# Strided attention in blocks of 18 tokens, V cast straight to its place, x turned on chip

## The chip, the cores and the metric

The kernel runs on one core of one Trainium2 chip. The core has five engines that run at the same time, each through its own instruction stream in order: PE (TensorE, matrix products into PSUM), DVE (VectorE), ACT (ScalarE), POOL (GpSimd) and SP (SyncE). They meet only through semaphores. SP and POOL compute nothing here: they issue DMAs. The metric is the device time in microseconds of one launch, as the median of several runs.

## The reference

An attention with two kinds of sparse masks, and after it a two-layer MLP with a rational function between the layers. There are 8 sequences (batches) of 576 tokens, 8 heads of 64 columns.

```python
stride = 32
scores = scale * np.matmul(q, k.transpose(0, 1, 3, 2))      # 8 x 8 x 576 x 576
rel = pos[:, None] - pos[None, :]
mask_local = (rel >= 0) & (rel < stride)                    # heads 0 to 3
mask_strided = (rel >= 0) & (pos[None, :] % stride == pos[:, None] % stride)   # heads 4 to 7
attn = softmax(np.where(mask, scores, -1e9))
x = (attn @ v) with heads side by side                      # 4608 x 512
h = x @ w_in                                                # 4608 x 2048
P = a[0] + a[1] * h + a[2] * h**2 + a[3] * h**3
Q = 1.0 + np.abs(b[0]) * np.abs(h) + np.abs(b[1]) * h**2
out = (P / (Q + 1e-06)) @ w_out                             # 4608 x 512
```

In a strided head, token t sees only tokens t, t - 32, t - 64 and so on: for each remainder of t by 32 there is a small attention of its own over 18 tokens.

## The kernel before

The program is written as a list of operations, each with an engine, a guessed duration, a key (its due time) and the tiles that it reads and writes. `schedule()` (line 124) places them in order of key on a model of the five engines, the PSUM banks and one DMA pipe, and so fixes each engine's stream; `emit()` (line 211) turns the dependences into semaphore waits. A DMA on SP or POOL that must wait holds all that stands behind it in that engine's stream.

For each batch b there are these stages.

- `casts(b)` (line 423, seven POOL DMAs): q, k and v are read as f32 and written as bf16 into DRAM. Local heads go in pairs to `lq16` and `lk16` (L428, 1,152 pieces of 128 B each), strided heads to `sq16` and `sk16` and all of v to `v16` (L436, long rows). The casts of b + 2 are released (`after`) by the first transpose of b + 1.
- `loads(b)` (line 464, on SP): four DMA transposes bring q and k into SBUF with the head dimension on partitions (`lqT`, `lkT` L469, `sqT`, `skT` L475). Then six loads put V for local heads into `vL` (L481, L486) and eight put V for strided heads into `vS` (L495), each of 36 partitions x 16 pieces of 128 B. `vL` and `vS` have a column of ones, so that AV also gives the row sum.
- `attention(b)`, local: a mask matmul (L509), 72 small score matmuls (L522), row maxima on DVE (L546), their subtraction by matmul (L553), exp on ACT to `pL` (L559, L563), a DMA transpose to `ptL` on SP (L566), 72 AV matmuls (L635).
- `attention(b)`, strided, two heads at a time (`j2`): blocks of 36 tokens, that is, remainders by 16, half of whose entries are masked. Mask (L578), 32 score matmuls of 64 x 36 (L591), maxima (L601), subtraction (L608), exp to `pS` (L614), transpose to `ptS` (L619); then 64 AV matmuls with P stationary (L687).
- `norm` (L655, L658) divides by the sums from PSUM into `xl` (local) and `xS` (strided). Stores from SP write these to `xs16` in DRAM (L665, L669, L696), and `gather` (L711) transposes them back into `xt`, a ring of two tiles of 512 tokens.

The MLP runs over nine chunks of 512 tokens (`mlp`, line 719). Each has 64 matmuls of 128 x 512 with W_in (L731), evacuated by ACT (L735) into two groups `h`; on each group |h| on ACT (L746) or DVE (L750), six bf16 passes on DVE (L753, L755, L768 to L776), Ln and Exp for the quotient on ACT (L759, L764); then 64 matmuls with W_out (L789), evacuated by ACT (L795) and stored by SP (L801).

The order at the start is casts(0), both halves of W_in, casts(1), both halves of W_out, all on POOL's queue without a wait between them. Attention of batch b has key 33 b - 20 and the MLP of chunk c key 33 c + 10, so attention(b + 1) is spread into mlp(b). After batch 7 two chunks, 7 and 8, are left with no attention beside them.

Of the kernel before, what the change touches and what calls it, by code (L numbers as in the profile page):

```python
# [305 lines left out]
def bass_strided_sparse_attn__then__act_rational_pade_kernel(nc, q, k, v, moe_w_in, moe_w_out, moe_a, moe_b, out):  # L306
# [59 lines left out]
    R_ptS = ring("ptS", 2, [128, 8, 112])  # L366
    R_xl = ring("xl", 1, [128, NLS])
    R_xS = ring("xS", 1, [128, 2048])
    R_ng = ring("ng", 4, [128, 18])
    R_rc = ring("rc", 4, [128, 18], f32)  # L370
    R_xt = ring("xt", 2, [128, NK1, CH])
# [51 lines left out]
    def casts(b, key, after=()):  # L423
        for t in (T_lq[b], T_lk[b], T_sq[b], T_sk[b], T_v[b]):
            t.new()

        def local(pair, s_t, d_t, t):
            P.op("pool", lambda e: e.dma_start(  # L428
                d_t[b, pair, :, :].rearrange("s (hh d) -> s hh d", hh=2),
                s_t[b, 2 * pair:2 * pair + 2, :, :].rearrange("hh s d -> s hh d")),  # L430
                2.8, key, w=[t], dma=(1.2, 3.0), after=after)

        def bulk(s_t, d_t, h0, nh, hd, t):
# [12 lines left out]
        bulk(v, vs, 0, H, H, T_v[b])  # L446

    def weights_in(i, key):
# [5 lines left out]
            2.8, key, w=[T_win[i]], dma=(5.5, 3.0))  # L454

    def weights_out(i, key, after=()):
# [4 lines left out]
            3.1, key, w=[T_wout[i]], dma=(5.5, 3.0), after=after)  # L461


    def loads(b, key):
        st = {}
        for nm, R, d_t, T in (("lq", R_lq, lq, T_lq), ("lk", R_lk, lk, T_lk)):
# [4 lines left out]
                1.25, key, r=[T[b]], w=[t], dma=(1.2, 2.2))  # L471
        for nm, R, d_t, T in (("sq", R_sq, sq, T_sq), ("sk", R_sk, sk, T_sk)):
# [4 lines left out]
                1.25, key + 0.1, r=[T[b]], w=[t], dma=(1.2, 2.2))  # L477
        vl = R_vL.next()
        st["vl"] = vl
        for hh in range(2):  # L480
            P.op("sp", lambda e, hh=hh: e.dma_start(  # L481
                vl.t[64 * hh + 32:64 * hh + 64, :, 0, 0:64],
                bass.AP(tensor=vs, offset=(b * H + hh) * S * D, ap=[[D, 32], [2 * S * D, 2], [1, D]])),
                0.5, key + 0.2, r=[T_v[b]], w=[vl], dma=(0.05, 2.0))
            for pair in range(2):
                P.op("sp", lambda e, hh=hh, pair=pair: e.dma_start(  # L486
                    vl.t[64 * hh:64 * hh + 64, pair, 1:NB, 0:64],
                    bass.AP(tensor=vs, offset=(b * H + 2 * pair + hh) * S * D,
                            ap=[[D, 64], [LB * D, NB - 1], [1, D]])),
                    0.5, key + 0.2, r=[T_v[b]], w=[vl], dma=(0.6, 2.0))  # L490
        vS = R_vS.next()
        st["vS"] = vS
        for r in range(2):
            for h in range(HL):
                P.op("sp", lambda e, r=r, h=h: e.dma_start(  # L495
                    vS.t[64 * r:64 * r + CS, h, :, 0:64],
                    bass.AP(tensor=vs, offset=(b * H + HL + h) * S * D, ap=[[16 * D, CS], [D, 16], [1, D]])),
                    0.7, key + 0.3, r=[T_v[b]], w=[vS], dma=(0.35, 2.0))
        return st


    def attention(b, st, key):
# [63 lines left out]
        P.op("sp", lambda e: e.dma_start_transpose(ptL.t[:, :, :], ppL.t[:, 0:NLS]), 1.25, key, r=[ppL], w=[ptL],  # L566
             dma=(1.1, 2.0))


        ptS = []  # L570
        for j2 in range(2):
            ky = key + 4 + 4 * j2
            SS = Banks(2)

            def smask(e, SS=SS):
                r = None
                for j in range(2):
                    r = e.matmul(bank(SS, 512 * j, 8 * CS), IDN[:, :],  # L578
                                 MS[:, :].unsqueeze(1).broadcast_to([128, 8, CS]),
                                 start=True, stop=False, skip_group_check=True)  # L580
                return r
            P.op("pe", smask, 0.25, ky, r=[T_c], w=[SS])

            def sscore(e, SS=SS, j2=j2):
                r = None
                for j in range(2):
                    h = 2 * j2 + j
                    for r2 in range(8):
                        for par in range(2):
                            p = 64 * par  # L590
                            r = e.matmul(bank(SS, 512 * j + CS * r2, CS, p, p + CS),  # L591
                                         sqt.t[p:p + 64, h, r2:S // 2:8], skt.t[p:p + 64, h, r2:S // 2:8],
                                         start=False, stop=True, skip_group_check=True)
# [276 lines left out]
```

## Time and profile before

| | us |
|---|---|
| Median of 3 runs | 594.68 |
| Lowest, highest | 588.09, 608.74 |
| The profiled execution | 588.41 |
| Its span in the trace | 586.60 |
| PE busy in the span | 349.3 |
| DVE busy | 314.7 |
| ACT busy | 306.6 |
| Moved by DMA | 62.71 MB in 213,187 packets |

The span runs from the first to the last instruction of the trace; 1.8 us of the measured time lie outside it. In the page's line of slices each digit is the busy share of a fortieth of the span in tenths. A row of a group gives line, engine, operation, output and inputs, shapes and count; then busy time, mean ns of one, and the idle time before it with what ended it. Matmuls overlap, so a group's busy time divided by its count says what one costs in a row. "SPq" is time in which SP's queue is issuing. The DMA share of a window can be over 1, since packets of two queues on one DMA engine overlap.

### The profile page before, as it was taken

The page shows a single profiled execution, that of the slowest core. Times are in us where ns is not written, and L with a number is a line of the kernel's source. Part 1 is how long each engine was busy: PE and PEld are TensorE (multiplying, and loading weights), DVE is VectorE, ACT ScalarE, POOL GpSimd, SP SyncE. Part 2 cuts the span into 40 slices and gives each one's busy share as a digit, 9 for nine tenths or more (in the row PEclk, how much of TensorE's full clock was granted, in tenths as well). Part 3 has the DMA queues.
Part 4 walks back from the last instruction along what each step waited for, and adds up shares of the span by engine and source line. Part 5 has one row for each costly group of instructions (what it writes and reads, how often), then busy time and mean ns, then how long its engine had stood idle before and what let it go on. Part 6 is the DMA issues. An engine that isn't in the chain of part 4 may idle for free.

```text
span 586.6 us, 7831 instructions
## 1 busy us (share of the span) xinstructions
PE 349.3 (60%) x3393; PEld 167.0 (28%) x3440; DVE 314.7 (54%) x227; ACT 306.6 (52%) x317; POOL 61.5 (10%) x64
## 2 busy tenths in 40 slices
PE   1012105103552379087796597994898899996846
PEld 0001004002221124043352244441443444442312
DVE  1001002201098807268694389393988789699781
ACT  0010001001373239188678465882986888999861
POOL 9200004013031031014004000000000000000000
PEclk9999999999985679699799779896998899998987
DMA  9999999979999999979959995795214414000101
GB/s 127 182 163 121 91 114 172 73 145 174 82 133 185 61 153 165 87 114 181 127 86 200 115 100 123 142 103 127 46 45 97 71 39 115 19 36 18 54 19 72
DMA packets 213187, 62.71 MB, mean 107 GB/s; under 512 B 196128, under 2 KB 207008, under 8 KB 212640
## 3 DMA queue, kind: packets, MB, share of 16 engines
q1 hardware_dynamic: 171744, 43.84, 57.2%
q0 software_dynamic: 41408, 18.35, 27.8%
q8 instruction: 27, 0.44, 0.3%
q14 instruction: 8, 0.07, 0.0%
HBM read 46.18 MB, written 28.31 MB: 127 GB/s over the span
## 4 chain that ended last, share of the span: by engine, by line
SPq 37%; PE 16%; DVE 16%; ACT 16%; DMA 12%; issue 4%; POOL 0%; ACTq 0%; POOLq 0%
SPq L495 10%; SPq L486 8%; PE ps L731 8%; PE ps L789 6%; DMA xt<-xs 5%; ACT z L746 5%; SPq L481 5%; DMA xs<-xS 4%; SPq L469 4%; SPq L475 4%; ACT h L735 4%; ACT u L759 3%; DVE u L755 3%; ACT u L764 2%; DVE z L770 2%
## 5 line engine op out<-in xcount | busy, mean ns | idle before, releaser
L731 PE MATMUL ps<-xt,Win 128*128 128x512 bf16 x554 | 149.1, 408 | 58.7 <-DMA xt<-xs 52.8
L789 PE MATMUL ps<-Wout,h 128*128 128x512 bf16 x553 | 149.9, 409 | 29.4 <-DVE h L776 17.0
L735 ACT ACTIVATE h<-ps 128x512 bf16<-128x512 f32 x144 | 82.0, 610 | 99.3 <-PE ps L731 98.4
L731 PEld LDWEIGHTS ps<-xt,Win 128*128 128x128 bf16 x576 | 56.3, 104 | 133.2 <-DMA xt<-xs 48.6
L789 PEld LDWEIGHTS ps<-Wout,h 128*128 128x128 bf16 x576 | 57.0, 104 | 101.5 <-DVE h L776 19.5
L759 ACT ACTIVATE u<-u,consts 128x2048 bf16<-128x2048 bf16 x36 | 70.6, 2000 | 19.3 <-DVE u L755 19.3
L764 ACT ACTIVATE u<-u 128x2048 bf16<-128x2048 bf16 x36 | 67.0, 1910 | 0.0
L428 POOL DMA_DIRECT2D lq<-in_q_dram x16 | 34.3, 2278 | 259.2 <-DMA lqT<-lq 258.4
L546 DVE TENSOR_REDUCE ng<-ps 128x18 bf16<-128x1152 f32 x8 | 10.8, 1356 | 93.5 <-PE ps L522 93.4
L746 ACT ACTIVATE z<-h 128x2048 bf16<-128x2048 bf16 x32 | 59.5, 1915 | 0.3
L522 PE MATMUL ps<-lkT,lqT 64*32 64x64 bf16 (+1 forms) x576 | 8.1, 207 | 79.6 <-DMA lkT<-lk 79.4
L753 DVE TENSOR_SCALAR u<-z,coef 128x4096 bf16<-128x4096 bf16 x18 | 24.1, 1338 | 58.2 <-ACT z L746 58.2
L559 ACT ACTIVATE pL<-ps 128x1024 bf16<-128x1024 f32 x8 | 8.2, 1019 | 79.9 <-PE ps L553 79.9
L776 DVE TENSOR_TENSOR h<-z,u 128x4096 bf16<-128x4096 bf16 x18 | 41.3, 2292 | 8.1 <-ACT u L764 7.6
L428 POOL DMA_DIRECT2D lk<-in_k_dram x16 | 41.6, 2923 | 0.0
L773 DVE TENSOR_TENSOR z<-z,h 128x4096 bf16<-128x4096 bf16 x18 | 41.2, 2291 | 0.5
L755 DVE TENSOR_TENSOR u<-u,z 128x4096 bf16<-128x4096 bf16 x18 | 41.1, 2283 | 0.4
L770 DVE TENSOR_TENSOR z<-z,h 128x4096 bf16<-128x4096 bf16 x18 | 40.9, 2272 | 0.3
L591 PE MATMUL ps<-skT,sqT 64*36 64x36 bf16 x512 | 20.2, 245 | 25.1 <-DMA skT<-sk 25.1
L795 ACT ACTIVATE os<-ps 128x512 f32<-128x512 f32 x36 | 21.5, 604 | 22.3 <-PE ps L789 22.2
L601 DVE TENSOR_REDUCE ng<-ps 100x16 bf16<-100x576 f32 x16 | 12.1, 755 | 35.8 <-PE ps L591 35.8
L522 PEld LDWEIGHTS ps<-lkT,lqT 64*32 64x32 bf16 x576 | 6.0, 94 | 86.9 <-DMA lkT<-lk 81.0
(39 smaller groups left out, 313.2 us busy)
## 6 DMA issues: line engine op xcount, KB each, us to landing
out_dram<-os SPq DMA_DIRECT2D x36, 256.0 KB, 2.7
v<-in_v_dram POOLq DMA_DIRECT2D x8, 576.0 KB, 13.1
vS<-v SPq DMA_DIRECT2D x64, 72.0 KB
vL<-v SPq DMA_DIRECT2D x32, 136.0 KB, 8.3
lq<-in_q_dram POOLq DMA_DIRECT2D x16, 144.0 KB, 7.4
lk<-in_k_dram POOLq DMA_DIRECT2D x16, 144.0 KB, 8.6
sq<-in_q_dram POOLq DMA_DIRECT2D x8, 288.0 KB, 9.6
sk<-in_k_dram POOLq DMA_DIRECT2D x8, 288.0 KB, 11.3
```

Source lines behind the costliest of these rows:

```text
L428: P.op("pool", lambda e: e.dma_start(d_t[b, pair, :, :].rearrange("s (hh d) -> s hh d", hh=2), s_t[b, 2 * pair:2 * pair + 2, :, :].rearran ...
L486: P.op("sp", lambda e, hh=hh, pair=pair: e.dma_start(vl.t[64 * hh:64 * hh + 64, pair, 1:NB, 0:64], bass.AP(tensor=vs, offset=(b * H + 2 * ...
L495: P.op("sp", lambda e, r=r, h=h: e.dma_start(vS.t[64 * r:64 * r + CS, h, :, 0:64], bass.AP(tensor=vs, offset=(b * H + HL + h) * S * D, ap= ...
L731: r = e.matmul(bank(ph, 0, CH), Win[:, kk, f * 128:(f + 1) * 128], xt.t[:, kk, :], start=(kk == 0), stop=(kk == NK1 - 1))
L735: P.op("act", lambda e, f=f, ph=ph, h=h: e.activation(h.t[:, f % G, :], bank(ph, 0, CH), AF.Copy), 0.597, ky, r=[ph], w=[h], occ=0.494)
L746: P.op("act", lambda e, z=z, h=h, i=i: e.activation(z.t[:, half * i:half * i + half, :], h.t[:, half * i:half * i + half, :], AF.Abs), 1.9 ...
L755: dv(lambda e, z=z, u=u: e.tensor_tensor(u.t[:, :, :], u.t[:, :, :], z.t[:, :, :], op=Alu.mult), 2.28, 4, r=[z], m=[u])
L759: lns.append(P.op("act", lambda e, u=u, i=i: e.activation(u.t[:, half * i:half * i + half, :], u.t[:, half * i:half * i + half, :], AF.Ln, ...
L764: exs.append(P.op("act", lambda e, u=u, i=i: e.activation(u.t[:, half * i:half * i + half, :], u.t[:, half * i:half * i + half, :], AF.Exp ...
L770: dv(lambda e, z=z, h=h: e.tensor_tensor(z.t[:, :, :], z.t[:, :, :], h.t[:, :, :], op=Alu.mult), 2.28, 8, r=[h], m=[z])
L776: dv(lambda e, z=z, h=h, u=u: e.tensor_tensor(h.t[:, :, :], z.t[:, :, :], u.t[:, :, :], op=Alu.mult), 2.28, 14, r=[z, u], m=[h])
L789: r = e.matmul(bank(po, 0, Fout), groups[g].t[:, j, m * 128:(m + 1) * 128], Wout[:, kk, :], start=(kk == 0), stop=(kk == NF - 1))
```

## The change

1. Strided attention works in 32 blocks of 18 tokens per head (remainders by 32) instead of 16 blocks of 36. All four heads go through one set of PSUM banks: 128 score matmuls of 64 x 18, packed in tiles of 64 rows x 32 columns, one maximum, one exp.
2. P is divided by its row sum before the AV product: exp writes f32 (`eS`), DVE sums it, takes the reciprocal and multiplies into bf16 `pS`. There is one transpose to `ptS` instead of two.
3. In the strided AV product V is stationary and P moves: 128 matmuls per batch, whose result has x already transposed. ACT copies one half of it and DVE the other into `XT`, a tile that holds the transposed x of all 4,608 tokens.
4. The local x is transposed from `xl` in SBUF into `XT` by four DMA transposes on SP. `xs16`, its stores, `gather` and `xt` are gone.
5. V is no longer cast to `v16` and loaded from there by SP. Ten POOL DMAs per batch cast it straight into `vS` (four, rows of 32 x 64) and `vL` (six).
6. What waits for what: W_in's first half is issued when `lqT` and `lkT` of batch 0 have landed, its second half when `ptL` has; casts(1), its V and W_out when `ptS` has. The casts and V of b + 2 are issued when all four transposes of b + 1 have landed (before: the first of them). Rings `xl` 1 to 2, `xS` gone.
7. Some durations of the planner's model are changed (`dma=`, `occ=`), and mask matmuls list the operands of the scores among their inputs.

```diff
+        vS = R_vS.next()
+        st["vS"] = vS
+        for h in range(HL):
+            P.op("pool", lambda e, h=h: e.dma_start(
+                vS.t[32 * h:32 * h + CS, :, :].rearrange("p r d -> p (r d)"),
+                v[b, HL + h, :, :].rearrange("(t r) d -> t (r d)", r=32)),
+                2.8, key, w=[vS], dma=(0.4, 2.5), after=after, occ=0.9)
...
-                P.op("sp", lambda e, hh=hh, pair=pair: e.dma_start(
+                P.op("pool", lambda e, hh=hh, pair=pair: e.dma_start(
                     vl.t[64 * hh:64 * hh + 64, pair, 1:NB, 0:64],
-                    bass.AP(tensor=vs, offset=(b * H + 2 * pair + hh) * S * D,
+                    bass.AP(tensor=v.tensor, offset=v.offset + (b * H + 2 * pair + hh) * S * D,
                             ap=[[D, 64], [LB * D, NB - 1], [1, D]])),
...
+                            r = e.matmul(bank(SS, 512 * par + CS * (4 * i + h), CS, 32 * b4, 32 * b4 + CS),
+                                         sqt.t[p:p + 64, h, c:S // 2:16], skt.t[p:p + 64, h, c:S // 2:16],
+                                         start=False, stop=True, skip_group_check=True, tile_position=(p, 32 * b4))
...
+        P.op("act", lambda e: e.activation(
+            eS.t[:, :].rearrange("p (j s) -> p j s", j=2),
+            PS[:, SS.at * 512:SS.at * 512 + 1024].rearrange("p (j c) -> p j c", j=2)[:, :, 0:16 * CS],
+            AF.Exp, scale=0.125), 0.68, ky, r=[SS], w=[eS], occ=0.58)
...
+        for pair in range(2):
+            P.op("sp", lambda e, pair=pair: e.dma_start_transpose(
+                XT[:, pair, t0:t0 + 512].rearrange("p (g c) -> p g c", g=4), xl.t[:, 512 * pair:512 * pair + 512]),
+                1.25, key, r=[xl], w=[T_xl[b][pair]], dma=(0.85, 2.0))
...
+                                r = e.matmul(bank(A, c, CS, 64 * hp, 64 * hp + 64),
+                                             vS.t[32 * h:32 * h + 32, 8 * b4 + 2 * i + par, :],
+                                             ptS.t[32 * h:32 * h + 32, 4 * par + i, 32 * b4:32 * b4 + CS],
+                                             start=True, stop=True, skip_group_check=True,
+                                             tile_position=(32 * h, 64 * hp))
...
+            def dst(pr):
+                return XT[:, 2 + pr, t0:t0 + S].rearrange("p (t j r) -> p j t r", j=2, r=16)
+            if pr == 0:
+                P.op("act", lambda e, A=A, pr=pr, src=src, dst=dst: e.activation(dst(pr), src(A), AF.Copy), 0.68, key,
+                     r=[A], w=[T_x[b]], occ=0.58)
...
+    QK = ("lq", "lk", "sq", "sk")
     casts(0, -100)
...
+    st = loads(0, -50)
+    vloads(0, -99, st)
+    weights_in(0, -95, after=landed(st, ("lq", "lk")))
+    attention(0, st, -20)
+    weights_in(1, -94, after=landed(st, ("ptL",)))
+    casts(1, -90, after=landed(st, ("ptS",)))
+    vst = {}
+    vloads(1, -89, vst, after=landed(st, ("ptS",)))
+    weights_out(0, -80, after=landed(st, ("ptS",)))
+    weights_out(1, -79, after=landed(st, ("ptS",)))
...
+        if b + 2 < B:
+            casts(b + 2, b * PER + 6, after=landed(st, QK))
+            vst = {}
+            vloads(b + 2, b * PER + 6.1, vst, after=landed(st, QK))
+        if b + 1 < B:
+            attention(b + 1, st, b * PER + PER - 20)
```

More of the change, by code (lines that the diff above doesn't have):

```diff
@@ L365, in bass_strided_sparse_attn__then__act_rational_pade_kernel @@
     R_pS = ring("pS", 2, [128, 1024])
[L366 to L371, printed above, removed]
+    R_ptS = ring("ptS", 2, [128, 8, 128])
+    R_xl = ring("xl", 2, [128, NLS + 16])
+    R_eS = ring("eS", 1, [128, 32 * CS], f32)
+    R_ng = ring("ng", 2, [128, 18])
+    R_nS = ring("nS", 2, [128, 32])
+    R_rc = ring("rc", 2, [128, 18], f32)
+    R_rS = ring("rS", 2, [128, 64], f32)
+    XT = sb("XT", [128, NK1, NT])
+    T_xl = [[Tile(f"xa{b}_{i}") for i in range(3)] for b in range(B)]
+    T_x = [Tile(f"x{b}") for b in range(B)]
     R_h = ring("h", 5, [128, G, CH])
@@ L423, in casts @@
     def casts(b, key, after=()):
-        for t in (T_lq[b], T_lk[b], T_sq[b], T_sk[b], T_v[b]):
+        for t in (T_lq[b], T_lk[b], T_sq[b], T_sk[b]):
             t.new()
@@ L445, in casts, with weights_in @@
         bulk(k, sk, HL, HL, HL, T_sk[b])
-        bulk(v, vs, 0, H, H, T_v[b])
-    def weights_in(i, key):
+    def weights_in(i, key, after=()):
         w = Fmid // 2
@@ L564, in attention @@
              0.3, key, r=[SL], w=[ppL], occ=0.2)
-        ptL = R_ptL.next()
+        ptL = st["ptL"] = R_ptL.next()
         P.op("sp", lambda e: e.dma_start_transpose(ptL.t[:, :, :], ppL.t[:, 0:NLS]), 1.25, key, r=[ppL], w=[ptL],
[L567 to L588, printed above, removed]
+             dma=(1.95, 2.0))
@@ new lines, in attention, with smask, sscore @@
+        ky = key + 4
+        SS = Banks(2)
+        def smask(e):
+            r = None
+            for par in range(2):
+                r = e.matmul(bank(SS, 512 * par, 16 * CS), IDN[:, :],
+                             MS[:, :].unsqueeze(1).broadcast_to([128, 16, CS]),
+                             start=True, stop=False, skip_group_check=True)
+            return r
+        P.op("pe", smask, 0.25, ky, r=[T_c, sqt, skt], w=[SS])
+        def sscore(e):
+            r = None
+            for i in range(4):
+                for h in range(HL):
+                    for b4 in range(4):
+                        c = 4 * b4 + i
@@ new lines, in sneg @@
+        def sneg(e):
+            r = None
+            for par in range(2):
+                r = e.matmul(bank(SS, 512 * par, 16 * CS), IDN[:, :],
+                             ngS.t[:, 16 * par:16 * par + 16].unsqueeze(2).broadcast_to([128, 16, CS]),
+                             start=False, stop=True, skip_group_check=True)
+            return r
+        P.op("pe", sneg, 0.25, ky, r=[ngS, T_c], m=[SS])
+        eS = R_eS.next()
+        P.op("act", lambda e: e.activation(
+            eS.t[:, :].rearrange("p (j s) -> p j s", j=2),
+            PS[:, SS.at * 512:SS.at * 512 + 1024].rearrange("p (j c) -> p j c", j=2)[:, :, 0:16 * CS],
+            AF.Exp, scale=0.125), 0.68, ky, r=[SS], w=[eS], occ=0.58)
@@ L623, in attention @@
+        ptS = st["ptS"] = R_ptS.next()
+        P.op("sp", lambda e: e.dma_start_transpose(ptS.t[:, :, :], ppS.t[:, :]),
+             1.25, ky, r=[ppS], w=[ptS], dma=(1.7, 2.0))
         key += 14
@@ L662, in attention, with accL @@
-        norm(AL, 3, 6, 128, lambda: xl.t[:, :], key, xl)
-        T_xs[b].new()
+        def accL():
+            return PS[:, AL.at * 512:(AL.at + 3) * 512].rearrange("p (j c) -> p j c", j=3)[
+                :, :, 0:390].rearrange("p j (s c) -> p j s c", c=65)
+        rc = R_rc.next()
+        P.op("dve", lambda e: e.reciprocal(rc.t[:, :].rearrange("p (j s) -> p j s", j=3).unsqueeze(3),
+                                           accL()[:, :, :, 64:65]), 0.29, key, r=[AL], w=[rc], occ=0.21)
```

208 lines of the change are left out of this document (76 added, 132 removed).

## The prediction

> **What bounds the kernel now.** I read the slices of the span first, then the chain that ended last.
>
> ```profile
> PE   1012105103552379087796597994898899996846
> ACT  0010001001373239188678465882986888999861
> DMA  9999999979999999979959995795214414000101
> SPq 37%; PE 16%; DVE 16%; ACT 16%; DMA 12%; issue 4%; POOL 0%; ACTq 0%; POOLq 0%
> SPq L495 10%; SPq L486 8%; PE ps L731 8%; PE ps L789 6%; DMA xt<-xs 5%; ACT z L746 5%; SPq L481 5%; DMA xs<-xS 4%; SPq L469 4%; SPq L475 4%; ACT h L735 4%; ACT u L759 3%; DVE u L755 3%; ACT u L764 2%; DVE z L770 2%
> ```
>
> A slice is 14.7 us. For ten slices the compute engines do almost nothing while the DMA engines are full. From slice 23 on DMA falls off and PE and ACT fill up. The chain spends 37% in SP's queue, 23% of it at L495, L486 and L481 (the loads of V from `v16`), and 9% in the two legs of the round trip through `xs16`. So the kernel has stages with different limits. The timeline of PE, at the first matmul of each MLP chunk, cuts them apart:
>
> ```profile
> 152.61 2.77 PE L731 MATMUL ps<-xt,Win 128*128 128x512 bf16 x6 [10.21 <-DMA xt<-xs]
> 208.87 1.89 PE L731 MATMUL ps<-xt,Win 128*128 128x512 bf16 x4 [12.48 <-DMA xt<-xs]
> 407.25 1.06 PE L731 MATMUL ps<-xt,Win 128*128 128x512 bf16 x2 [8.80 <-DMA xt<-xs]
> 449.19 1.02 PE L731 MATMUL ps<-xt,Win 128*128 128x512 bf16 x2 [1.85 <-DMA xt<-xs]
> 491.93 1.24 PE L731 MATMUL ps<-xt,Win 128*128 128x512 bf16 x5
> ```
>
> Chunk 0 starts at 152.61, chunk 7 at 491.93, the span ends at 586.6. So it is a start of 152.6 us, seven periods (one chunk and one batch of attention each) of 339.3/7 = 48.5 us, and a tail of 94.7 us (two chunks, no attention). Early periods take 56 us (152.61 to 208.87), late ones 42, and what ends PE's wait at each start is the transpose out of `xs16`. Busy time in the first 150 us, in two late periods and in the tail:
>
> ```profile
> core 0: us, PE busy (x) PEld busy (x) DVE busy (x) ACT busy (x) POOL busy (x), PEclk, DMA share, GB/s
> 0.00:150.00 150.00, 26.55 (x620) 17.07 (x622) 14.66 (x24) 8.32 (x13) 31.46 (x36) 1.00 1.24 135
> 407.00:449.00 42.00, 37.45 (x408) 17.76 (x414) 34.30 (x25) 34.14 (x35) 0.00 (x0) 0.94 0.31 73
> 449.00:491.00 42.00, 38.73 (x339) 18.57 (x345) 33.28 (x26) 35.28 (x37) 0.00 (x0) 0.92 0.29 66
> 491.00:540.00 49.00, 43.36 (x197) 19.23 (x200) 41.87 (x24) 47.01 (x48) 0.00 (x0) 0.98 0.14 43
> ```
>
> In a late period PE is busy for 37 to 39 of 42 us, ACT for 35, DVE for 34: little room there. In the tail ACT is busy for 47 of 49 us, so this program can pack an engine to 96% where nothing waits for a transfer. I price the three terms one by one.
>
> **Start: from 152.6 to about 50 us.** The timeline shows what the first batches wait for (the two last rows are of the DMA issues: KB each, median us to landing):
>
> ```profile
> 1.29 1.48 POOL L428 DMA_DIRECT2D lq<-in_q_dram  x1 [0.84 <-POOLq L855]
> 8.91 5.49 SPq L469 DMA_TRANSPOSE lqT<-lq  x1
> 20.04 9.98 SPq L475 DMA_TRANSPOSE sqT<-sq  x1
> 63.45 12.51 SPq L495 DMA_DIRECT2D vS<-v  x8
> 76.01 4.14 SPq L566 DMA_TRANSPOSE ptL<-pL  x1
> 83.23 1.42 SPq L469 DMA_TRANSPOSE lqT<-lq  x1
> 32.57 0.91 PE L522 MATMUL ps<-lkT,lqT 64*32 64x64 bf16 x72 [26.67 <-DMA lkT<-lk]
> 38.33 0.27 ACT L563 ACTIVATE pL<-ps 128x128 bf16<-128x128 f32 x1
> 55.35 2.40 PE L591 MATMUL ps<-skT,sqT 64*36 64x36 bf16 x64 [15.55 <-DMA skT<-sk]
> Win<-in_moe_w_in_dram POOLq DMA_DIRECT2D x2, 1024.0 KB, 19.8
> ptL<-pL SPq DMA_TRANSPOSE x8, 4.9
> ```
>
> The first casts of q and k have landed at 8.91. Issuing a transpose takes 5.5 to 10 us there against 1.42 at 83.23, because POOL has put both batches' casts and all four weight halves onto its queue at once. Then the 14 loads of V hold SP until 76, and `ptL`, whose P is ready at 39, goes out behind them at 76. The change takes all 14 off SP and sends V by ten POOL DMAs. It also holds W_in's first half until `lqT` and `lkT` have landed, its second until `ptL`, and batch 1's casts and W_out until `ptS`.
>
> After the first casts POOL's queue then has ahead of any weight: two bulk casts, four V DMAs of 72 KB, six for `vL`. The first local cast went out at 1.29, and `lqT` could go at 8.91, when the first and third of the four had landed: 3,456 rows of 128 B in 7.6 us with their latency. `vL` has 4,480 rows of that size: at most 9.9 us. 288 KB of `vS` and twice 288 KB of bulk at the 135 GB/s of the first 150 us are 6.4; by then it is about 25 us. So the cover the old order gave W_in (it came early) is gone; W_in must travel while attention(0) computes. I put `lkT` at 18 us (the ends: 9 + 2 x 1.4 + 2 = 14; 32.6 as now) and `skT` at 26 (16; 55 as now). Local: scores to exp took 32.57 to 38.6, 6 us, so `ptL` goes out at 24 and lands at 29. Strided: 2.4 us for 64 matmuls, up to 4.8 for 128, then maximum, minus, exp, sum, reciprocal and product, at most 0.7 each (L614 below): P at 35, `ptS` landed at 40, AV and the copies 3 us: x at 43 to 45. Landing medians are 4.9 us for `ptL` and 19.8 for a half of W_in: its first half is there at 38, its second at 49, when f < 8 still runs. I take 50; the ends are 42 and, if transposes land as late as today, 55 + 17 = 72.
>
> **Period: from 48.5 to 39 us.** What each part adds or takes away per batch, from the groups:
>
> ```profile
> L591 PE MATMUL ps<-skT,sqT 64*36 64x36 bf16 x512 | 20.2, 245 | 25.1 <-DMA skT<-sk 25.1
> L687 PE MATMUL ps<-vS,ptS 36*64 36x65 bf16 (+1 forms) x512 | 13.6, 217 | 16.0 <-DMA ptS<-pS 8.4 <-issue 7.1 <-ACT pS L614 0.4
> L635 PE MATMUL ps<-vL,ptL 64*32 64x65 bf16 x576 | 8.7, 210 | 11.3 <-ACT h L735 10.6 <-ACT pL L563 0.6
> L578 PE MATMUL ps<-MS,IDN 128*128 128x288 bf16 x32 | 8.0, 345 | 2.6 <-ACT pL L563 0.8 <-DVE xS L658 0.8 <-ACT os L795 0.7
> L658 DVE TENSOR_TENSOR xS<-ps,rc 100x1152 bf16<-100x1152 f32 (+1 forms) x16 | 19.3, 1217 | 0.0
> L614 ACT ACTIVATE pS<-ps 100x576 bf16<-100x576 f32 x16 | 10.4, 666 | 20.3 <-PE ps L608 20.3
> ```
>
> - PE, strided scores: 64 matmuls at 20.2/512 = 39 ns (2.5 us) become 128 narrower ones. Ends: 15 ns each as in the tiled L635 (1.9 us) and 39 ns (5.0). The operands stay strided as in L591, the packing becomes L635's: I take the middle, 3.4, +0.9.
> - PE, strided AV: 64 at 13.6/512 = 27 ns (1.7 us) become 128 at 15 to 27 ns, 1.9 to 3.4; middle +0.9. Masks and maxima: four matmuls of 288 columns each become two: four fewer at 8.0/32 = 0.25 us, -1.0. PE net +0.8 (ends -1.5 to +3.2).
> - ACT: two exps of 576 elements become one, and one copy of 576 elements out of PSUM is new: 0.67 against 0.67, nothing.
> - DVE: two maxima of 576 elements become a maximum and a sum, nothing. The products over `xS`, 19.3/8 = 2.4 us, and two reciprocals go; a reciprocal, a product over 576 elements and a copy of 576 come, by L658 some 0.7 each for the two last. DVE -1.0 us; it isn't the fullest.
> - SP: 14 loads and five stores go; of 4 + 1 + 2 + 2 transposes, the four of `xl` replace the two of `xt`, and one `ptS` goes. Ten transposes at 1.4 us are 14 us per batch, the `out` stores add 2; hidden in 39, unless `xl` queues behind a transpose that is not yet released.
> - POOL: seven issues become 16. Their spacing is 0.8 us in the rows further down (265.08 to 265.86), so 13 us in a period of 39. The new wait stands ahead of the casts of b + 2, for all four transposes of b + 1: the V loads queue behind it, and only attention(b + 2) waits for them, a whole period later.
> - The trip through `xs16` goes: x is written to `XT` by transposes on chip and by the two copies. The 8.80 us before 407.25 go with it. Late next is whichever engine is fullest.
>
> So the period is bounded below by ACT's 35.3 and above by the 42 of today; PE's 38.73 + 0.8 = 39.5 is the fullest. With fewer gaps PEclk should rise a little from 0.92 toward the tail's 0.98, so I take 39. [...]
>
> **Tail: 94.7 us, kept.** No attention in it, ACT-bound, and no line of it changes.
>
> **Sum.** 50 + 7 x 39 + 94.7 = 417.7 us of span, plus 588.41 - 586.60 = 1.8 around it: 419.5, say **420 us**. The median of the runs, 594.68, lies 6.3 above the profiled one; that is inside my range.
>
> **Rivals.**
>
> *DMA sets the pace of the periods.*
>
> ```profile
> DMA packets 213187, 62.71 MB, mean 107 GB/s; under 512 B 196128, under 2 KB 207008, under 8 KB 212640
> q1 hardware_dynamic: 171744, 43.84, 57.2%
> q0 software_dynamic: 41408, 18.35, 27.8%
> ```
>
> q1 takes 335.5 us for 171,744 packets. By counting rows, some 97,800 go net (V's loads 72,700, `xs` and `xt` 28,200, narrower `ptS` 6,100, against 9,200 for `xl`): 144 us stay. q0 takes 163 us for 41,408 and gains 35,840 rows of `vL`: up to 304 us. 448 us of packet time, at the share of 1.24 that the first 150 us sustained (its window, above), is 361 us, 45 per batch: 50 + 7 x 45 + 94.7 + 1.8 = **462 us**. Against it: those prices contain the waiting of two full queues on each other; the first local casts, with little beside them, took 7.6 us for 3,456 rows, and `vL` at that price adds 9.9 us a batch, not 141/8 = 17.6.
>
> *POOL sets the pace.*
>
> ```profile
> 263.26 2.89 POOL L428 DMA_DIRECT2D lk<-in_k_dram  x1
> 265.08 2.42 POOL L428 DMA_DIRECT2D lq<-in_q_dram  x1
> 265.86 3.80 POOL L428 DMA_DIRECT2D lk<-in_k_dram  x1
> 263.24 1.43 DVE L772 TENSOR_SCALAR z<-z,coef 128x4096 bf16<-128x4096 bf16 x1
> 264.71 2.29 DVE L773 TENSOR_TENSOR z<-z,h 128x4096 bf16<-128x4096 bf16 x1
> ```
>
> One issue came 1.8 us after the one before instead of 0.8, as an L772 ran; the next was not held by L773. If every one of 16 waited for a 2.29 us op it would be 16 x 3.1 = 49 us per batch, **490 us**. [...]
>
> *Only the start is won:* PE's small matmuls take the upper price and the periods stay at 42: **441 us**. *All packs:* start 42, periods at ACT's 35.3: **386 us**.
>
> *Slower than before.* The cast of b + 2 waits for transposes of b + 1, which wait for casts of b + 1: a loop that no compute covers if it grows. Today's periods of 42 to 56 us hold that loop too. It makes the kernel slower by 2% only if a batch takes (594.68 x 1.02 - 50 - 94.7 - 1.8)/7 = 65.7 us or more, say 68: **622 us**. Nothing in the profile shows transposes or casts at twice today's loaded times, with fewer packets in the queues.
>
> **How the numbers follow.** My forecast (periods of 37 to 41) 0.52; only the start 0.17; all packs 0.10; DMA 0.12; POOL 0.05; slower 0.04. The likeliest alone would be 405 to 437. The range reaches to both neighbours and, with a late start, the DMA case: 386 to 480. About 2% can be told from no change: faster 0.95, same 0.01, slower 0.04.
>
> **What would show it.** Right: the first L731 (its new line) near 50 us; SP's queue under 10% of the chain; chunk starts 37 to 41 us apart; PE, ACT and DVE over 85% busy from the first chunk on; L591's successor near 27 ns; the last 95 us as before. Wrong: PE waiting for `XT` in mid-span with SP's queue as releaser, chunk starts tied to POOL's bursts, or `skT` of batch 0 landing after 40 us.

## The result, and the profile after

The changed kernel takes 477.86 us (median of four runs, 469.70 to 481.49) against 591.38 us for the kernel before, run beside it: a ratio of 0.800, 95% interval 0.787 to 0.814. The ratio and its interval take the faster runs of each kernel alone, and the profiled execution, 479.66 us with a span of 477.9, is one of the slower two of the four.

The slices and the chain that ended last, of the changed kernel (a slice is now 11.9 us):

```profile
PE   0023792474787586999895597998988999989647
ACT  0002175430239659789865297697987899999861
PEclk9999995579779567999969697999998999998778
DMA  9999999999999999999999999963022010011102
PE 28%; DMA 28%; ACT 20%; DVE 15%; SPq 4%; issue 3%; POOL 1%; ACTq 0%; POOLq 0%
PE ps L790 10%; PE ps L732 10%; DMA lkT<-lk 7%; DMA ptS<-pS 7%; ACT u L760 6%; ACT u L765 5%; ACT z L747 4%; DMA skT<-sk 4%; DMA XT<-xl 4%; PE ps L693 3%; ACT h L736 3%; SPq L466 3%; DMA lq<-in_q_dram 2%; DVE z L774 2%; DMA out_dram<-os 2%
```

SP's queue has gone from 37% of the chain to 4%, and PE has work from the fifth slice on. But DMA is still full for 26 of 40 slices, until about 311 us, and transfers have grown from 12% of the chain to 28%. The chunks now start at 54.4, 135.2, 170.9, 205.4, 268.6, 301.9, 339.0 and 379.1 us (first matmul of L732 of each). Busy time between some of these starts:

```profile
core 0: us, PE busy (x) PEld busy (x) DVE busy (x) ACT busy (x) POOL busy (x), PEclk, DMA share, GB/s
54.40:135.20 80.80, 49.27 (x746) 21.19 (x746) 39.08 (x27) 30.29 (x34) 32.27 (x41) 0.77 1.67 135
135.20:205.40 70.20, 56.06 (x779) 26.93 (x780) 51.92 (x38) 52.78 (x54) 26.86 (x32) 0.78 1.71 114
205.40:268.60 63.20, 48.60 (x770) 24.17 (x769) 44.20 (x31) 45.26 (x47) 25.54 (x30) 0.86 1.68 132
268.60:301.90 33.30, 30.75 (x309) 14.51 (x310) 28.26 (x19) 26.16 (x30) 15.29 (x16) 0.86 1.58 127
301.90:339.00 37.10, 35.26 (x539) 17.15 (x538) 30.78 (x22) 31.50 (x33) 0.00 (x0) 1.00 0.64 82
339.00:379.00 40.00, 36.80 (x539) 17.64 (x538) 34.33 (x25) 34.41 (x37) 0.00 (x0) 0.96 0.18 49
```

| term | before | forecast | after |
|---|---|---|---|
| start (to the first MLP matmul) | 152.6 | 50 | 54.4 |
| seven periods | 339.3 | 273 | 324.7 |
| tail | 94.7 | 94.7 | 98.8 |
| span | 586.6 | 417.7 | 477.9 |

So the gain is almost wholly the start. Five periods take 33 to 40 us, as forecast or less; two take 81 and 63 us. These two cost 66 us more than 2 x 39, which is more than the whole miss. The DMA queues, and the landing of two kinds of transposes (KB left out for transposes; median us from issue to landing):

```profile
q0 software_dynamic: 79168, 20.59, 65.2%
q1 hardware_dynamic: 72096, 25.88, 46.0%
lqT<-lq SPq DMA_TRANSPOSE x8, 14.7
lkT<-lk SPq DMA_TRANSPOSE x8, 16.6
```

q0 is POOL's queue: 0.652 x 477.9 = 311.6 us of packet time of all 16 DMA engines, against 163.1 before; in the mean over all packets 3.94 ns, just as before. q1, SP's, has 219.8 us, against 335.5 before. Together that is 531 us; over the first 320 us the DMA share is 1.60. What this does in the first period stands in the timeline of DVE, SP and PE:

```profile
54.42 16.59 PE L732 MATMUL ps<-XT,Win 128*128 128x512 bf16 x64 [1.01 <-DMA XT<-xl]
108.55 0.74 DVE L623 TENSOR_TENSOR pS<-eS,rS 128x576 bf16<-128x576 f32 x1
108.28 4.44 SPq L472 DMA_TRANSPOSE sqT<-sq  x1
112.76 5.99 SPq L672 DMA_TRANSPOSE XT<-xl  x2
118.80 2.63 SPq L629 DMA_TRANSPOSE ptS<-pS  x1
129.21 2.10 PE L693 MATMUL ps<-ptS,vS 32*64 32x18 bf16 x128 [1.33 <-issue]
135.26 5.09 PE L732 MATMUL ps<-XT,Win 128*128 128x512 bf16 x16
```

P of batch 1 is ready at 109.3. Its transpose goes out at 118.8, behind a load of batch 2 and the transposes of x, of which each holds SP for 3 to 4.4 us, where the `skT` issued at 124.02 held it for 1.36. AV runs at 129, chunk 1 at 135. But SP is not what ended last: `ptS` has landed at 124.1, 5 us before AV. These are links of the chain that ended last, from the list of its pieces in order of time (start, us, what); the last line is of the second long period:

```profile
72.78 18.56 DMA skT<-sk
94.68 8.47 DMA lk<-in_k_dram
103.17 15.86 DMA lkT<-lk
119.07 1.04 PE ps L508 x2
129.21 2.10 PE ps L693 x127
251.26 17.28 DMA XT<-xl
```

Batch 1's `skT` takes 18.6 us from issue to landing. The casts of batch 2 wait for it (POOL, 91.64), and then their `lkT` takes 15.9. PE stands at 119.07 at L508, the mask of batch 2, which waits for that `lkT` and is ahead of batch 1's AV (L693) in PE's stream. So late transposes of the next batch hold up this one, by way of PE's order. The 63 us period ends with a transpose of x into `XT` that takes 17.3 us to land; the median of these is 4.5. In that period the scores of L590 also stand still for 9.66 us, for which the profile names no releaser.

### The profile page after: what moved, and what is told of

It reads as the page before. It is cut to its first block, busy times and chain, and to the rows that moved or that the text cites. A ratio compares the mean times of both kernels' runs of the same rounds, so it can differ in the third digit from the quotient of the medians.

```text
span 477.9 us, 9780 instructions
## 1 busy us (share of the span) xinstructions
PE 348.7 (73%) x4432; PEld 163.2 (34%) x4432; DVE 314.3 (66%) x219; ACT 305.6 (64%) x317; POOL 119.1 (25%) x136
## 3 DMA queue, kind: packets, MB, share of 16 engines
q0 software_dynamic: 79168, 20.59, 65.2%
q1 hardware_dynamic: 72096, 25.88, 46.0%
## 4 chain that ended last, share of the span: by engine, by line
PE 28%; DMA 28%; ACT 20%; DVE 15%; SPq 4%; issue 3%; POOL 1%; ACTq 0%; POOLq 0%
PE ps L790 10%; PE ps L732 10%; DMA lkT<-lk 7%; DMA ptS<-pS 7%; ACT u L760 6%; ACT u L765 5%; ACT z L747 4%; DMA skT<-sk 4%; DMA XT<-xl 4%; PE ps L693 3%; ACT h L736 3%; SPq L466 3%; DMA lq<-in_q_dram 2%; DVE z L774 2%; DMA out_dram<-os 2%
## 5 line engine op out<-in xcount | busy, mean ns | idle before, releaser
L790 PE MATMUL ps<-Wout,h 128*128 128x512 bf16 x576 | 155.1, 411 | 21.0 <-DVE h L777 12.6
L732 PE MATMUL ps<-XT,Win 128*128 128x512 bf16 x576 | 153.3, 407 | 7.7 <-ACT h L736 3.8
L732 PEld LDWEIGHTS ps<-XT,Win 128*128 128x128 bf16 x576 | 55.3, 103 | 83.7 <-issue 15.6
L426 POOL DMA_DIRECT2D lq<-in_q_dram x16 | 32.9, 2059 | 141.4 <-DMA skT<-sk 133.3
L494 POOL DMA_DIRECT2D vL<-in_v_dram x32 | 54.2, 3075 | 0.0
L489 POOL DMA_DIRECT2D vL<-in_v_dram x16 | 41.1, 2764 | 3.1 <-PE ps L645 3.1
L426 POOL DMA_DIRECT2D lk<-in_k_dram x16 | 39.6, 2621 | 0.0
L508 PE MATMUL ps<-M,IDN 128*128 128x512 bf16 x16 | 6.5, 500 | 44.6 <-DMA lkT<-lk 44.6
L482 POOL DMA_DIRECT2D vS<-in_v_dram x32 | 34.9, 2661 | 5.8 <-PE ps L693 5.8
L693 PE MATMUL ps<-ptS,vS 32*64 32x18 bf16 x1024 | 21.6, 184 | 16.0 <-DMA ptS<-pS 13.9
## 6 DMA issues: line engine op xcount, KB each, us to landing
Win<-in_moe_w_in_dram POOLq DMA_DIRECT2D x2, 1024.0 KB, 10.1
```

The lines of the kernel that those rows point to most:

```text
L426: P.op("pool", lambda e: e.dma_start(d_t[b, pair, :, :].rearrange("s (hh d) -> s hh d", hh=2), s_t[b, 2 * pair:2 * pair + 2, :, :].rearran ...
L494: P.op("pool", lambda e, hh=hh, pair=pair: e.dma_start(vl.t[64 * hh:64 * hh + 64, pair, 1:NB, 0:64], bass.AP(tensor=v.tensor, offset=v.off ...
L732: r = e.matmul(bank(ph, 0, CH), Win[:, kk, f * 128:(f + 1) * 128], XT[:, kk, c * CH:c * CH + CH], start=(kk == 0), stop=(kk == NK1 - 1))
L790: r = e.matmul(bank(po, 0, Fout), groups[g].t[:, j, m * 128:(m + 1) * 128], Wout[:, kk, :], start=(kk == 0), stop=(kk == NF - 1))
```

## The experiments

Theory A: the DMA engines' small pieces, above all those on POOL's queue, set the pace until the casts are done. Theory B: it is the order in which the in-order streams and the releases put the work. Every edit but e2's also makes the planner order the streams anew, so only e2 parts the two cleanly. Ratios are to the kernel before, with 95% intervals; the changed kernel has 0.800 (0.787 to 0.814).

**e1: each V row cast once.** A row of V stands in `vL` twice, on both halves of 64 partitions; here the second copy is made by DVE.

```diff
-                    vl.t[64 * hh:64 * hh + 64, pair, 1:NB, 0:64],
+                    vl.t[64 * hh + 32:64 * hh + 64, pair, 0:NB, 0:64],
...
+            P.op("dve", lambda e, hh=hh: e.tensor_copy(
+                vl.t[64 * hh:64 * hh + 32, :, 1:NB, 0:64], vl.t[64 * hh + 32:64 * hh + 64, :, 0:NB - 1, 0:64]),
+                0.75, key, m=[vl], occ=0.67)
```

> Each V row of the local heads is cast once (four DMAs of 32 partitions x 18 rows, 2,304 pieces of 128 B per batch instead of 4,416), and two DVE copies of 2,176 elements per batch shift it to the other 32 partitions. The output is the reference's. Theory A (the DMA engines' small pieces set the pace up to about 316 us): 8 x 2,112 = 16,900 pieces fewer at 311.6 us / 79,168 = 3.9 ns is 67 us of packet time, about 40 us of wall at a share of 1.6; the casts end 35 to 45 us earlier and the time falls by 15 to 35 us, to 440 to 460. Theory B (the order of the in-order streams and the releases sets the early periods, DMA only fills the gaps): the first period stays near 81 us and the time within 10 us of 475.

453.5 us, 0.767 (0.762 to 0.771). Theory A's range. Its queues:

```profile
q0 software_dynamic: 61504, 18.36, 48.0%
q1 hardware_dynamic: 72096, 25.88, 37.3%
```

Packet time falls to 216 + 168 = 384 us. SP's queue has the same packets as in the changed kernel, and yet its packet time falls, from 219.8 to 168 us. Over the traces with these packets on SP's queue it is 182 to 220 us where all pieces of `vL` are on POOL's queue (the changed kernel, e3, e4, e8, e11), 168 to 182 with about half of them (e1, e6, e7) and 161 in e2: with fewer of POOL's pieces SP's same packets take less time (219.8 against 161 us, where e2 keeps the order), and the order counts as well. But the first period stays at 77 us, as theory B had it.

**e2: nearly no vL from batch 2 on.**

```diff
-                    vl.t[64 * hh:64 * hh + 64, pair, 1:NB, 0:64],
+                    vl.t[64 * hh:64 * hh + 64, pair, 1:NB if b < 2 else 2, 0:64],
...
-                            ap=[[D, 64], [LB * D, NB - 1], [1, D]])),
+                            ap=[[D, 64], [LB * D, NB - 1 if b < 2 else 1], [1, D]])),
```

> From batch 2 on the four vL casts carry one block of 64 rows instead of 17, so local heads of batches 2 to 7 use stale V; every instruction, its order and every wait stay. 24,600 pieces fewer of 79,168 on POOL's queue. Theory A: some 97 us of packet time or 60 us of wall go, DMA ends near 255 us, the periods after the first fall to about 36 us and the time to 430 to 445. Theory B: the time stays within 10 us of 475, since no release and no order is changed.

449.6 us, 0.761 (0.756 to 0.767). No order and no release changed, so theory B alone is out: by the ratios the pieces left out are worth 23 us. But theory A expected 430 to 445: 7,000 pieces fewer than e1 brought almost nothing more.

**e3: masks that wait for constants alone.**

```diff
-        P.op("pe", lmask, 0.49, key, r=[T_c, lqt, lkt], w=[SL])
+        P.op("pe", lmask, 0.49, key, r=[T_c], w=[SL])
...
-        P.op("pe", smask, 0.25, ky, r=[T_c, sqt, skt], w=[SS])
+        P.op("pe", smask, 0.25, ky, r=[T_c], w=[SS])
```

> The two mask matmuls depend on the constants alone again, as before the change. Theory A says nothing of it: within 10 us of 475. Theory B in its form that the mask's wait for lkT (44.6 us of PE in the trace) is itself a loss: 10 to 25 us faster. Against both, the planner may then take PSUM banks for the scores long before they are needed and hold up the MLP: its own planned span rises from 420 to 449, which would give some 500 us.

490.5 us, 0.823 (0.816 to 0.831): this small part of the change is worth 13 us. The first scores of batches 1 and 2 and the first MLP matmul in e3:

```profile
77.44 0.86 PE L521 MATMUL ps<-lkT,lqT 64*32 64x64 bf16 x72 [36.41 <-DMA lkT<-lk]
123.57 0.86 PE L521 MATMUL ps<-lkT,lqT 64*32 64x64 bf16 x72 [16.82 <-DMA lkT<-lk]
128.48 1.75 PE L732 MATMUL ps<-XT,Win 128*128 128x512 bf16 x4
```

Chunk 0 starts at 128.5 us instead of 54.4. In PE's stream the planner now puts the scores of batches 1 and 2 ahead of chunk 0, and each stands there for its `lkT`. In the kernel before, whose masks wait for constants too, it is the same: the scores of batches 1 and 2 (L522) run at 88.7 and 131.2, chunk 0 at 152.6. With every other part of the change in place and this one undone, the start is only 24 us earlier than before. So the order of PE's stream, by way of part 7, is needed for most of the start's gain. The first period is 40 us in e3, and so most of what the start loses comes back there. That the masks hold PSUM banks early, as was expected, no run shows.

**e4: batch 1's casts released earlier**, by the four transposes of batch 0.

```diff
-    casts(1, -90, after=landed(st, ("ptS",)))
+    casts(1, -94.5, after=landed(st, QK))
...
-    vloads(1, -89, vst, after=landed(st, ("ptS",)))
+    vloads(1, -94.4, vst, after=landed(st, QK))
```

> casts(1) and its V are released by the four transposes of batch 0 (about 35 us) instead of ptS of batch 0 (50 us), ahead of W_in's second half. Theory A: DMA is full either way, W_in's second half comes later; within 10 us of 475. Theory B: the first period falls by about the 15 us that the release comes earlier, from 81 to 65 us, and the time to about 460.

473.1 us, 0.800 (0.797 to 0.804): the same. Chunk 0 starts later (73.7), chunk 1 earlier (126.8), chunk 3 at 208 as against 205. The release only moves the wait, as theory A has it.

**e5: V by way of `v16` and SP again**, in the new layouts.

```diff
+        bulk(v, vs, 0, H, H, T_v[b])
...
-            P.op("pool", lambda e, h=h: e.dma_start(
+            P.op("sp", lambda e, h=h: e.dma_start(
                 vS.t[32 * h:32 * h + CS, :, :].rearrange("p r d -> p (r d)"),
-                v[b, HL + h, :, :].rearrange("(t r) d -> t (r d)", r=32)),
+                vs[b, HL + h, :, :].rearrange("(t r) d -> t (r d)", r=32)),
```

> One part undone: V is cast in long rows to v16 in DRAM and loaded by SP, as before the change, but into the new layouts (four loads of long rows into vS, six of 128 B pieces into vL). All else is the changed kernel. Theory A (it is the count of small pieces that costs, on whichever queue): the 4,480 pieces of vL only change queue and the detour adds some 30 long packets a batch; 470 to 490 us. Theory C (casting V straight is what relieved the start, since SP's queue filled up with V's loads): ten more issues on SP stand between the transposes, the start rises from 54 to over 70 us and the time to over 500.

455.7 us, 0.768 (0.758 to 0.779): 22 us faster than the changed kernel by the medians, 19 by the ratios, and the intervals do not touch. Theory A counted pieces and had no change here; theory C had a loss. Both are wrong. Queues and landing:

```profile
q1 hardware_dynamic: 109568, 32.83, 46.3%
q0 software_dynamic: 41408, 18.35, 37.7%
lqT<-lq SPq DMA_TRANSPOSE x8, 4.3
```

The number of packets is the same as in the changed kernel (151 thousand), more bytes are moved, and yet packet time falls from 531 to (0.463 + 0.377) x 456.6 = 384 us. `lqT` lands in 4.3 us instead of 14.7. So the count of pieces is not what costs: V's pieces are dearer as a cast on POOL's queue, and the transposes beside them land later. That is plainest for batch 0, whose q and k are cast in the same way in the changed kernel, in e1 and in e5. PE's first mask, which waits for `lkT`, in this order:

```profile
31.41 1.03 PE L508 MATMUL ps<-M,IDN 128*128 128x512 bf16 x2 [31.41 <-DMA lkT<-lk]
25.02 1.03 PE L504 MATMUL ps<-M,IDN 128*128 128x512 bf16 x2 [25.02 <-DMA lkT<-lk]
19.92 1.03 PE L511 MATMUL ps<-M,IDN 128*128 128x512 bf16 x2 [19.92 <-DMA lkT<-lk]
```

With all of `vL`'s pieces behind the casts on POOL's queue `lkT` lands at 31.4 us, with about half of them at 25.0, with none at 19.9. As it stands, part 5 of the change is a loss. How much of the 19 to 22 us is V's pieces and how much the new order, e5 alone does not tell.

**e6: e1 with the copies later in DVE's stream**, behind the local exp.

```diff
-                0.75, key, m=[vl], occ=0.67)
+                0.75, key - 2, m=[vl], occ=0.67, after=ppL.w)
```

The copies now stand behind the line `key += 14`, so `key - 2` is 12 later than in e1.

> As e1_v_once, but the two DVE copies stand behind the local exp in DVE's stream (they depend on it), so that DVE no longer waits for vL in front of MLP work. Theory A: same transfers as e1; the first period loses the 12 us for which PE waited for DVE there; 440 to 452 us against 453.5. If that wait only hid another one (the landing of ptL and of batch 2's lkT), it stays at 450 to 457.

450.4 us, 0.765 (0.758 to 0.772). Within e1's interval, and inside both expected ranges, so it decides nothing.

**e7 and e8: another order.** The planner's model takes every transfer 1.25 times as long, in e6 and in the changed kernel.

```diff
                 us, lat = o.dma
+                us *= 1.25
```

> As e6, with every transfer time in the planner's model times 1.25, so that the streams are ordered for later landings; same operations, pieces and releases. Theory B (order matters beside the pieces): 10 to 20 us under e6. Theory A alone: within 5 us of e6.

> The changed kernel with every transfer time in the planner's model times 1.25; same operations, pieces and releases, only the order in the five streams is another. Theory B: the streams no longer put batch b + 2's loads ahead of batch b + 1's P and x; the first period falls from 81 to 65 us or less, the time by 15 to 30 us. Theory A: DMA is full up to some 315 us as before; within 8 us of 474.

e7: 467.3 us, 0.793 (0.784 to 0.802), 17 us slower than e6, where one side expected 10 to 20 us faster and the other no change. e8: 469.2 us, 0.797 (0.788 to 0.805), not told apart from the changed kernel. So order alone can cost 17 us, and this way of changing it does not mend the first period: 80.7 us in e7, 73.1 in e8.

**e9: meant as the best.** `vS` cast straight, local V by way of `v16` and SP, each row once, with the copies of e6.

```diff
+        bulk(v, vs, 0, HL, HL, T_v[b])
...
+                P.op("sp", lambda e, hh=hh, pair=pair: e.dma_start(
+                    vl.t[64 * hh + 32:64 * hh + 64, pair, 0:NB, 0:64],
+                    bass.AP(tensor=vs, offset=(b * HL + 2 * pair + hh) * S * D,
+                            ap=[[D, 32], [LB * D, NB], [1, D]])),
```

> Meant to beat both kernels. vS is cast straight as in the change (72 long rows a batch); the local heads' V goes in long rows to v16 and from there by SP, each row once (2,304 pieces of 128 B a batch), and two DVE copies shift it to the other 32 partitions. Packet time by e5's prices (1.9 ns of all engines per piece on SP's queue, 3.9 on POOL's) falls by 4,416 x 3.9 - 2,304 x 1.9 = 13 us a batch against the changed kernel. Theory A (packet time sets the pace until the casts are done): 430 to 447 us. If what is left is order and computation: 447 to 457, like e5 and e6.

452.5 us, 0.773 (0.758 to 0.788); packet time (0.395 + 0.365) x 451.3 = 343 us. Not under e5 and e6: packet time does not set the pace here, as the second expectation had it.

**e10: the kernel before with the releases alone.**

```diff
+    weights_in(0, -95, after=landed(st, ("lq", "lk")))
+    attention(0, st, -20)
+    weights_in(1, -94, after=landed(st, ("ptL",)))
+    casts(1, -90, after=landed(st, ("ptS",)))
```

> The kernel before with the change's releases alone (W_in by lqT and lkT, and by ptL; batch 1's casts and W_out by ptS; the casts of b + 2 by four transposes). If the releases carry the start: chunk 0 starts at 80 to 100 us instead of 152 and the time falls by 30 to 60 us, to 530 to 560. If the start was held by V's 14 loads on SP and by DMA being full: chunk 0 stays over 120 us and the time over 575.

557.0 us, 0.953 (0.941 to 0.966). Chunk 0 starts at 121.2 instead of 152.6. The first scores of batch 1 and the first MLP matmul:

```profile
82.45 0.86 PE L522 MATMUL ps<-lkT,lqT 64*32 64x64 bf16 x72 [49.60 <-DMA lkT<-lk]
121.20 1.89 PE L731 MATMUL ps<-xt,Win 128*128 128x512 bf16 x4 [23.03 <-DMA xt<-xs]
```

The two expectations split: the time is that of the releases, the start, by 1 us, that of the other side. Alone the releases give 31 us of the start's 98. Here too PE stands for 49.6 us at batch 1's scores, ahead of batch 0's AV (L635 at 87.2), which is e3's order. V leaving SP's queue is not needed for the start: e5 has V's loads on SP and starts at 55.0. No run parts the strided blocks, whose V needs 72 long rows a batch instead of 4,608 pieces, from x on chip.

**e11: the changed kernel without its releases at the start.**

```diff
-    weights_in(0, -95, after=landed(st, ("lq", "lk")))
+    weights_in(0, -95)
```

> The changed kernel without its releases at the start: W_in, batch 1's casts and V, and W_out are issued as soon as POOL gets to them. Theory A: the same transfers, DMA full either way; chunk 0 starts late (100 to 130 us), but the following periods are short, and the time stays within 15 us of 474. If the releases are worth what the start shows: 510 to 560 us.

483.0 us, 0.829 (0.817 to 0.841). The first MLP matmul:

```profile
98.22 4.62 PE L732 MATMUL ps<-XT,Win 128*128 128x512 bf16 x16
```

Chunk 0 comes 44 us later, chunk 1 at 133.1, where it was with the releases (135.2). So most of what the releases win at the start is given back in the first period. 3 to 4% of the time are kept. That is theory A's side, with chunk 0 a little ahead of its 100 to 130 us.

**e12: q and k of the local heads in long rows too**, laid side by side by SP.

```diff
+        bulk(q, q16, 0, HL, HL, T_q16[b])
...
-            P.op("pool", lambda e: e.dma_start(
+            P.op("sp", lambda e: e.dma_start(
                 d_t[b, pair, :, :].rearrange("s (hh d) -> s hh d", hh=2),
```

> e9 with q and k of the local heads cast in long rows too, and laid side by side by SP in bf16 (four DRAM to DRAM transfers of 1,152 pieces a batch). 4,608 pieces a batch change from POOL's queue to SP's. By e5's prices 4,608 x 2 = 9 us of packet time a batch go, against one more hop of some 4 us before each transpose and four more issues on SP. Theory A: 10 to 20 us under e9. If the hop or SP's queue decides: 5 to 30 us over e9.

455.9 us, 0.784 (0.767 to 0.801): not told apart from e9, and neither expectation, though packet time falls again:

```profile
q1 hardware_dynamic: 128416, 32.96, 43.9%
q0 software_dynamic: 5952, 18.36, 22.5%
```

Packet time of both queues (shares times span) against the median time:

| kernel | packet time, us | time, us | chunk 1, first weight load |
|---|---|---|---|
| changed | 531 | 477.9 | 135.2 |
| e3 | 510 | 490.5 | 168.3 |
| e8 | 502 | 469.2 | 131.1 |
| e11 | 497 | 483.0 | 133.1 |
| e4 | 478 | 473.1 | 126.8 |
| e7 | 397 | 467.3 | 132.2 |
| e5 | 384 | 455.7 | 122.6 |
| e1 | 384 | 453.5 | 123.8 |
| e6 | 384 | 450.4 | 122.6 |
| e2 | 346 | 449.6 | 125.5 |
| e9 | 343 | 452.5 | 125.6 |
| e12 | 301 | 455.9 | 115.5 |

The first five make the same transfers, and their times, 469 to 490 us, do not follow their packet time. Six runs with 384 us or less lie at 450 to 456, whatever their packet time; e7, with the pieces of e6 in another order, lies at 467. So fewer pieces on POOL's queue go with some 20 us less, once, and order makes about as much. The best with the reference's whole computation is e6 at 450.4 us, with e1, e5 and e9 within its interval or close by.

## Why the prediction was right, and where it was wrong

The direction came as reasoned, and the start and the tail came out near their numbers. The time, 477.9, lies at the very end of the range (480): the likeliest case was 58 us too fast, and the time came out past the rival "DMA sets the pace of the periods" (462). That it lies inside is luck: the range was drawn to reach the DMA case with a late start, and the start was not late, and the periods were not 45 us each but five of 33 to 40 and two of 63 and 81. Of the signs named, SP's share of the chain (4%) and the first L732 near 50 us came; chunk starts 37 to 41 us apart and engines over 85% busy from the first chunk on did not (PE is 61% busy in the first period).

- *Start, 50 us: the number right (54.4), the way to it only in part.* SP's queue is gone from the chain, and W_in travels beside attention(0). But the steps came later than priced: `lkT` of batch 0 at 31.4 (forecast 18), `ptS` at 50.0 (40), x at 54 (43 to 45); the 50 held because it was put some 5 us behind x, for W_in's second half. And neither V nor the releases carry it alone: the releases by themselves bring chunk 0 to 121 us (e10), without them it stands at 98 (e11), and without the masks' new operands, which the working does not mention, at 128.5 (e3).
- *Period, 39 us: the step that failed* (46.4 in the mean). The sum went over engines, and over engines it holds: in the two periods without casts PE is busy for 35.3 and 36.8 us, ACT for 31.5 and 34.4, and they last 37.1 and 40.0. What failed is that the transfers were taken as hidden: in the two long periods the chain runs through transposes that take 16 to 19 us to land. One term behind it was mis-sized, the price of V's small pieces. I had both: 3.94 ns per packet on POOL's queue, the mean of the profile before, which made up to 304 us for that queue, and the unloaded price of the first casts. I chose the second. Measured are 311.6 us, the first one to 3%, but not because each piece costs that (last section). On SP's queue I had 144 us left and 220 were measured: beside POOL's pieces its 72,096 packets took 3.05 ns each, where the mean before was 1.95. The 1.24 that I took as the share that DMA can sustain was 1.6 to 1.7. The pieces explain some 23 us (e2) of the 52 by which the seven periods exceed the forecast; the cause of the rest, most of it in the first period, stays open.
- *"SP ... hidden in 39, unless xl queues behind a transpose that is not yet released":* something near the exception came, in the first period, for `ptS`: SP stood at transposes that had been released but took two to three times the 1.4 us priced. It was not what ended the wait there: `ptS` had landed 5 us before PE came to it.
- *V straight into the blocks costs nothing (POOL: 13 us a batch): wrong.* POOL's own time is 15 us a batch (119 us in all), near the 13 priced, but the pieces behind it cost some 23 us (e2).
- *PE's small matmuls: fair.* From the groups after:

```profile
L693 PE MATMUL ps<-ptS,vS 32*64 32x18 bf16 x1024 | 21.6, 184 | 16.0 <-DMA ptS<-pS 13.9 <-issue 1.3 <-ACT XT L708 0.7
L590 PE MATMUL ps<-skT,sqT 64*18 64x18 bf16 x1024 | 10.7, 201 | 14.1 <-issue 14.1
L576 PE MATMUL ps<-MS,IDN 128*128 128x288 bf16 x16 | 3.9, 334 | 0.0
L623 DVE TENSOR_TENSOR pS<-eS,rS 128x576 bf16<-128x576 f32 x8 | 6.0, 756 | 0.2
L711 DVE CAST XT<-ps 128x576 bf16<-128x576 f32 x8 | 6.1, 757 | 21.2 <-PE ps L693 21.2
L708 ACT ACTIVATE XT<-ps 128x576 bf16<-128x576 f32 x8 | 5.2, 650 | 24.6 <-PE ps L693 24.6
```

  Scores cost 10.4 ns each (forecast 27), AV 21 (forecast 20), the masks half. The copies into `XT` cost 0.65 and 0.76 us, as priced.
- *PEclk:* 1.00 and 0.96 in the two late periods, where PE is busy for 95 and 92% of the time, and 0.77 in the first, where it is busy for 61%. But it is 0.86 both from 205.4 to 268.6 us (PE 77% busy) and from 268.6 to 301.9 (92%), and 1.00 in the first 54.4 us, where PE is busy for 10.1. That it rises with fewer gaps, for which I took 39 and not 39.5, was my estimate from three windows of the profile before; no run shows it.
- *POOL sets the pace: no.* POOL is idle for three quarters of the span (busy for 119.1 of 477.9 us). DVE's passes beside POOL's issues:

```profile
92.09 2.18 DVE L769 TENSOR_SCALAR z<-h,coef 128x4096 bf16<-128x4096 bf16 x1
92.44 2.62 POOL L426 DMA_DIRECT2D lk<-in_k_dram  x1
96.63 1.29 DVE L773 TENSOR_SCALAR z<-z,coef 128x4096 bf16<-128x4096 bf16 x1
L769 DVE TENSOR_SCALAR z<-h,coef 128x4096 bf16<-128x4096 bf16 x18 | 25.5, 1416 | 0.5
```

  This L769 took 2.18 us beside POOL's issues; all 18 of them take 1.42 in the mean (last row). But L773, of the same kind, took its usual 1.29 us among POOL's issues 4 us later, so these rows do not settle whether POOL's issues lengthen DVE's passes.
- *Tail, 94.7: nearly* (98.8). The runs with the changed attention have tails of 96 to 100 us; none tells where the 4 us come from.

What stays open is the first period. It takes 68 to 81 us in the changed kernel, e1, e2, e5, e6 and e9; where chunk 0 starts later, it is shorter, and chunk 1 starts between 115 and 135 us in every kernel with the changed attention but e3. Fewer pieces (e2, e9, e12), earlier casts (e4), no releases (e11) and another order (e8) each moved it by 20 us at most. By the trace of the changed kernel, batch 1's last transpose of q and k lands only at 91.4, PE stands 7.6 us for W_out's transfer until 90.4, and batch 1's AV then comes behind batch 2's masks. Whether W_out's transfer beside the casts, the chain of cast, transpose, scores and P itself, or PE's order sets this, no run separates.

## What to carry to other kernels

Before a load is moved to another queue to save a hop, do not price its pieces at the rate of an idle queue (here the first casts' 7.6 us for 3,456 rows), and ask what shares the DMA engines with them. Here V's small pieces, cast on the way into SBUF, were dear (5.2 to 5.4 ns of all 16 engines each, by e2 and e1), and the transposes beside them landed late (`lqT` after 14.7 us in the median, in e5 after 4.3); casting V in long rows and cutting it afterwards was faster (e5, 455.7 us against 477.9). For q and k the same step bought nothing (e12, 455.9 us against e9's 452.5). Then look at what stands ahead in PE's stream: here work of the next batch that waited for a transpose held up this batch's work behind it (L508 stood for 5.9 us until 119.07, ahead of batch 1's AV at 129.21). And where a start is won, see when the second chunk comes: with the releases chunk 0 came 44 us earlier than in e11, and chunk 1 2 us later (135.2 against 133.1).

## What the runs showed of the hardware

- POOL's queue took 3.94 ns of all 16 engines per packet in the kernel before (163.1 us for 41,408) and again in the changed one (311.6 for 79,168), but that mean is not the price of a piece. e1 and e2 have 17,664 and 24,576 packets of `vL` fewer than the changed kernel, and POOL's queue 95.6 and 127.2 us less: 5.4 and 5.2 ns each. e12 has 36,864 packets fewer than e9, of q and k cast into DRAM, and 62.7 us less: 1.7 ns each, net of the long rows that take their place. Whether it is the way into SBUF or the fuller queue that makes `vL`'s dearer, no run separates. SP's queue took 1.95 ns per packet before and 1.93 in e5 (211.4 us for 109,568).
- The same four q and k transposes per batch: the median landing of `lqT` was 11.7 to 14.7 us in the five kernels with all of `vL`'s pieces on POOL's queue, 9.7 to 12.7 in the three with about half of them (e1, e6, e7), 6.2 in e2 and 4.3 to 8.1 in the three with none (e5, e9, e12).
- DMA's packet time was 1.58 to 1.71 times the wall time in the windows from 54 to 302 us, more than the 1.24 of the first 150 us before.
